# Windowed attention and a two-layer feed-forward: one more chunk's up product from seven quarter products, in a new order

## The chip, the core and the metric

The kernel runs on one core of a Trainium2 chip. The metric is the device time of one execution in microseconds (us); three runs of the kernel before took 290.29, 290.93 and 291.28, median 290.93. Engines: PE (TensorE, matrix products; its weight loads are listed as PEld), DVE (VectorE), ACT (ScalarE), POOL (GpSimd) and SP (SyncE, which here only issues DMAs). Each engine runs its own instructions in the order in which they were recorded, and waits on semaphores for the others.

## The reference

Attention over 8 batches, 8 heads, 576 positions and head size 64, where each position sees itself and the 63 before it; its output, as 4608 tokens of 512, goes through a feed-forward layer with a quick Gelu.

```python
scores = scale * np.matmul(q, k.transpose(0, 1, 3, 2))
rel = pos[:, None] - pos[None, :]
mask = (rel >= 0) & (rel < 64)
scores = np.where(mask, scores, -1e9)
attn = softmax(scores)                      # over the last axis
x = np.matmul(attn, v)                      # to [4608 tokens, 512]
h = x @ w_in                                # 512 -> 2048
g = h * (1.0 / (1.0 + np.exp(-1.702 * h)))
return (g @ w_out).astype(np.float32)       # 2048 -> 512
```

## The kernel before

**Tiling.** The 4608 tokens are 9 chunks (0 to 8) of 512, each of four blocks of 128 tokens (m = 0 to 35). A block m holds two query blocks of 64; batch b has nine of these.

**Order.** There is no loop. One long text, `plan`, lists every step by a short name, and a loop at its end calls one small function a step (table `steps`, L728). The list's order is the order of each engine's queue. A step's place among another engine's steps says nothing about its time: only the order on its own engine and the waits do.

**Attention steps.** `lb.b.i.q` (or k, v): POOL issues the load of 128 rows of q, k or v as bf16 (L227). `y.b.i.w`: SP issues a DMA transpose of such rows into `qt` or `kt` (L241; w = 0 is q, 1 is k). `h.b.i.p`: POOL shifts v by half a block into `v_off` (L234). `c.m`: scores of block m on PE (L301, matmuls L318), into the PSUM pool S or two of the pools a to d. `x.m`: exp on ACT (L326), preceded by a load of the activation table where the last function was Gelu. `m.m`: mask on DVE. `v.m.2.tag`: the products with v for blocks m and m+1 on PE (L372, L346). `n.m.2`: normalization on DVE (L383). `xd.m`: SP issues the DMA transpose of the result into `xT` (L433), the input of the feed-forward part.

**Up product, plain.** `u.ch.f.2.t0.256.tag` computes two of the sixteen 128-wide parts of h for 256 tokens: 8 matmuls of 256 columns into one PSUM bank (L441, L447). `e...` empties the bank by a Gelu on ACT (L477); a few units use `t` (tanh on ACT) and `g` (DVE) instead. In chunks 1 and 2 a unit holds four parts for 128 tokens: 16 matmuls of 128 columns.

**Up product, from seven quarter products.** Chunk 8 is computed by Strassen's scheme (with Winograd's sums). Group g = 4 ch + 2 h + k (chunk 8: 32 to 35) holds four 128x512 results: two halves of the outputs by two halves of the tokens. `F.g.n` (L645, matmuls L658) is product n, 4 matmuls of 256 columns. Products 1, 6, 7, 4 add up in one PSUM bank (`UA`), 2, 5 and 3 use another (`UB`): 5 overwrites 2, and 3 is added to 5. `K.g.n` (L670) copies `UA` after products 1, 6 and 7 to SBUF in f32, on ACT or DVE; PE's next product into that bank waits for the copy. `O.g.n` (L673) on DVE adds such a copy to `UB` after 2, 5 and 3, into one of two slots (`s_homes`, table `slots`, L638), and `G.g.n` (L680, L684) on ACT makes the Gelu of the slot, or for n = 4 of the bank itself. The sums of weights are made by `aw` (DVE, 8 of them), the sums of x by `ax.ch.n` (DVE, 4 a chunk; their places for chunks 7 and 8 are in `x_sums`, L599).

**Down product.** Chunks 1 to 8 use the same scheme for the second layer: `a` (DVE, sums of g, L529), `p.q.n` (PE, 8 matmuls of 256 columns, L543, L559; q = 2 ch + half), `k` (copy of a chain, L578), `o` (DVE, sum to the output tile, L581), `z` (last copy, L587), `s` (store, by SP or ACT, L572).

**PSUM.** Pools S and T have two banks, a to d one each. A step that names a pool waits until the last tile in it has been read.

The table of slots and the two places of the plan that matter most (L638, and from L833 on):

```python
slots = {(g, n): i % 2 for i, (g, n) in enumerate(
    ((32, 2), (33, 2), (33, 5), (32, 5), (32, 3), (33, 3))
    + ((34, 2), (35, 2), (35, 5), (34, 5), (35, 3), (34, 3)))}
```

Of the kernel before, what the change touches and what calls it, by code (L numbers as in the profile page):

```python
# [28 lines left out]
def kernel(  # L29
# [597 lines left out]
    def add_x(ch, n):  # L627
# [12 lines left out]
        for i, (g, n) in enumerate(  # L640
            ((32, 2), (33, 2), (33, 5), (32, 5), (32, 3), (33, 3))
            + ((34, 2), (35, 2), (35, 5), (34, 5), (35, 3), (34, 3))
# [81 lines left out]
    def hold(n):  # L724
# [108 lines left out]
        YY.10.0.A u.2.12.4.128.128.b w.1.0 YY.10.1.A lb.3.4.k h.2.4.0 lb.4.4.v y.2.3.1 c.12 h.3.0.0  # L833
        u.2.0.4.256.128.c u.2.8.4.256.128.b y.3.0.1 e.2.12.128 u.2.8.4.384.128.c w.3.1 e.2.0.256
        cv.2.2.2.P e.2.8.256 w.2.0 lb.3.3.q u.2.0.4.384.128.b u.2.12.4.256.128.c lb.3.4.q a.2.3
        e.2.8.384 w.4.0 e.2.0.384 e.2.12.256 w.3.0 lb.4.1.q a.2.1 u.2.12.4.384.128.b y.3.0.0 h.2.3.0
        e.2.12.384 w.1.1 a.3.3 a.3.1 lb.4.0.v a.2.2 w.2.1 a.3.2 k.2.1.A h.2.3.1 lb.3.2.v ds.0.2.S
        u.2.4.4.256.128.c u.2.4.4.384.128.b p.2.6 y.2.4.1 lb.4.0.k e.2.4.256 lb.3.3.v y.2.4.0
        p.3.1.c o.2.2.i a.2.4 y.3.1.0 k.3.1.V y.3.2.1 p.3.2.b a.3.4 lb.4.1.k e.2.4.384 p.3.6 y.3.2.0
        k.2.6.A p.2.7 c.13 x.12 o.3.2.f k.2.7.A k.3.6.V p.3.7 x.13 k.3.7.A w.4.1 p.2.4 p.3.5 m.12  # L840
        m.13 v.12.2.a z.2.A.g n.12.2 p.3.4 p.2.5 XX.12.T y.3.4.1 y.3.4.0 o.3.5.h y.3.3.1 z.3.V
# [17 lines left out]
        e.4.6.0 e.4.4.0 y.5.0.0 u.4.14.2.0.256.a e.4.12.0 u.4.0.2.0.256.d x.21 k.6.1.V x.20 p.6.6  # L859
        m.20 u.4.2.2.256.256.c k.6.6.V s.4.0.N.S h.4.1.1 y.5.0.1 s.5.0.N.S h.5.1.1 lb.5.1.q y.5.1.0  # L860
        m.21 lb.5.1.k u.4.10.2.256.256.d y.5.1.1 e.4.0.0 u.4.4.2.256.256.a y.5.2.0 e.4.14.0
        e.4.10.256 h.4.3.0 lb.5.4.k p.6.7 k.6.7.V lb.6.0.v e.4.4.256 h.4.2.0 v.20.2.d n.20.2
        e.4.2.256 c.22 x.22 m.22 p.6.4 u.4.8.2.256.256.a p.6.2.c z.6.A.g t.4.8.256 u.4.0.2.256.256.d
        o.6.2.e xd.20 p.6.5 lb.5.3.q y.5.3.0 lb.5.0.v p.7.1.b xd.21 e.4.0.256 u.4.14.2.256.256.d
        a.7.2 a.7.4 u.4.12.2.256.256.a g.4.8.256 k.7.1.A e.4.14.256 p.7.6 lb.6.1.q h.5.0.0 o.6.5
        p.6.3 k.7.6.V c.23.da s.6.1.N.S c.24 p.7.7 y.6.1.0 o.6.3 e.4.12.256 lb.6.0.q x.23 m.23
        y.6.0.0 a.8.3 lb.5.3.v h.5.0.1 y.5.4.1 k.7.7.A p.7.2.c u.5.14.2.0.256.d o.7.2.i x.24 c.25
        x.25 h.5.1.0 v.22.2.a lb.6.1.v p.7.5 lb.6.3.k n.22.2 xd.23 lb.6.1.k u.5.4.2.0.256.a e.5.14.0
        o.7.5.g xd.22 p.7.4 e.5.4.0 h.5.3.0 m.24 u.5.12.2.0.256.d e.5.12.0 u.5.10.2.0.256.a lb.6.0.k
        p.7.3 o.7.3 y.6.0.1 e.5.10.0 lb.5.2.v u.5.8.2.0.256.d e.5.8.0 y.6.1.1 u.5.6.2.0.256.a z.7.A  # L870
        s.7.1.N.S u.5.0.2.0.256.c e.5.0.0 a.8.1 p.8.1.d h.5.3.1 k.8.1.V a.8.2 m.25 u.5.2.2.0.256.b
        e.5.2.0 u.4.6.2.256.256.c h.6.1.0 s.5.1.N.S lb.6.2.k lb.6.4.k e.4.6.256 lb.6.2.v p.8.6
        k.8.6.A lb.5.4.q u.5.8.2.256.256.b a.9.3 a.9.1 u.5.12.2.256.256.c h.5.2.1 y.5.4.0 e.5.6.0
        e.5.12.256 h.5.2.0 v.24.2.a lb.7.2.k lb.6.2.q c.27 p.8.7 k.8.7.A n.24.2 lb.7.0.v xd.25 a.8.4
        e.5.8.256 a.10.3 p.9.1.c a.10.1 u.5.2.2.256.256.a k.9.1.V e.5.2.256 a.9.2 lb.7.0.q
        u.5.6.2.256.256.b x.27 t.5.6.256 lb.6.4.q p.8.4 z.8.V.g s.3.1.N.S lb.7.0.k p.8.2.a o.8.2.f
        u.5.4.2.256.256.d p.9.6 xd.24 h.6.2.1 a.9.4 p.8.5 h.6.0.0 g.5.6.256 y.6.4.1 y.7.0.0
        u.5.0.2.256.256.b o.8.5 h.6.2.0 y.6.2.1 k.9.6.V e.5.4.256 e.5.0.256 p.8.3 o.8.3 p.9.7
        k.9.7.V m.27 c.26 x.26 lb.7.1.q c.28.db m.26 s.8.1.N.S u.5.14.2.256.256.a lb.5.4.v x.28
        p.9.4 z.9.V.h a.10.2 a.10.4 e.5.14.256 u.6.6.2.0.256.d lb.7.1.k u.5.10.2.256.256.b e.6.6.0  # L880
        p.10.1.c k.10.1.V e.5.10.256 a.11.3 a.11.1 lb.6.3.q u.6.2.2.0.256.a p.9.2.d o.9.2.g h.5.4.0
        e.6.2.0 u.6.4.2.0.256.b e.6.4.0 y.7.0.1 u.6.12.2.0.256.a e.6.12.0 m.28 lb.7.2.q lb.6.3.v
        p.10.6 k.10.6.A u.6.10.2.0.256.b y.6.4.0 a.11.2 p.9.5 h.7.0.1 y.6.3.1 o.9.5 e.6.10.0 p.10.7
        k.10.7.A p.9.3 y.6.2.0 v.26.2.a c.29 x.29 c.31.bd x.31 s.6.0.N.S o.9.3 n.26.2
        u.6.8.2.0.256.a p.10.4 p.10.2.b m.29 h.6.3.0 u.6.0.2.0.256.d o.10.2.e p.10.5 z.10.V.f
        e.6.8.0 lb.6.4.v o.10.5 y.7.1.0 e.6.0.0 h.6.1.1 s.8.0.N.S h.6.0.1 v.28.2.a h.7.0.0 y.6.3.0
        c.30 y.7.1.1 c.32.cd x.32 x.30 p.10.3 lb.7.3.v n.28.2 o.10.3 m.32 xd.27 p.11.1.a aw.1.0
        lb.7.4.q u.6.14.2.0.256.c k.11.1.A aw.1.1 xd.26 m.30 e.6.14.0 a.12.3 u.6.12.2.256.256.d
        u.6.4.2.256.256.b e.6.4.256 e.6.12.256 lb.7.4.k p.11.6 k.11.6.V u.6.10.2.256.256.c
        t.6.10.256 u.6.2.2.256.256.b t.6.2.256 p.11.7 g.6.10.256 u.6.14.2.256.256.d m.31  # L890
        u.6.6.2.256.256.c s.9.0.N.S e.6.14.256 g.6.2.256 xd.29 h.6.4.0 y.7.2.1 y.7.2.0 k.11.7.V
        h.6.3.1 v.30.2.b n.30.2 s.10.0.N.S lb.7.1.v c.33 x.33 u.6.0.2.256.256.d t.6.0.256 p.11.4
        z.11.A.g p.11.2.b aw.2.0 g.6.0.256 xd.28 u.7.2.2.0.256.a u.6.8.2.256.256.d o.11.2.e h.7.3.1
        e.6.6.256 lb.7.3.k y.7.3.1 u.7.10.2.0.256.c h.7.1.1 a.11.4 p.11.5 e.7.2.0 lb.7.3.q lb.7.2.v
        lb.7.4.v h.7.2.0 m.33 y.7.4.1 h.7.1.0 v.32.2.a e.6.8.256 a.13.3 o.11.5 y.7.3.0 c.34 y.7.4.0
        c.35.dc e.7.10.0 x.34 h.7.4.0 x.35 n.32.2 p.11.3 o.11.3 u.7.0.2.0.256.a u.7.12.2.0.256.b
        e.7.12.0 u.7.4.2.0.256.d h.7.3.0 m.35 xd.31 h.7.2.1 u.7.6.2.0.256.c m.34 v.34.2.b e.7.0.0
        e.7.6.0 a.12.1 e.7.4.0 xd.30 p.12.1.a u.7.8.2.0.256.c u.7.2.2.256.256.d k.12.1.A s.11.0.N.S
        a.12.2 s.7.0.N.S xd.33 p.12.6 aw.4.0 n.34.2 u.7.6.2.256.256.b k.12.6.V p.12.7 xd.32 F.32.1.S
        F.32.2.T t.7.2.256 g.7.2.256 e.7.8.0 e.7.6.256 u.7.14.2.0.256.c aw.2.1 a.13.1 e.7.14.0  # L900
        aw.4.1 p.13.1.d k.13.1.V u.7.14.2.256.256.b u.7.12.2.256.256.c k.12.7.A p.12.4 a.12.4 a.13.2
        a.13.4 p.13.6 e.7.12.256 u.7.4.2.256.256.c e.7.14.256 aw.3.0 k.13.6.A z.12.A.e xd.35
        K.32.1.A F.33.1.b p.12.2.a xd.34 ax.8.3 ax.8.1 ax.8.2 F.32.6 O.32.2 s.10.1.N.S a.14.3 a.14.1
        K.33.1.A F.33.6 e.7.4.256 ax.8.4 o.12.2.i F.32.5 K.32.6.A p.13.7 F.32.7 p.12.5 k.13.7.V
        p.13.4 K.33.6.V F.33.7 u.7.8.2.256.256.c K.33.7.A F.33.2.d o.12.5 p.12.3 G.32.2 z.13.V.f
        s.9.1.N.S O.33.2 F.33.4 K.32.7.A o.12.3 s.12.1.N.A F.32.4 G.33.2 e.7.8.256 p.13.2.a o.13.2.h
        F.33.5 O.33.5 G.33.4 u.7.10.2.256.256.c O.32.5 e.7.10.256 p.13.5 aw.3.1 o.13.5 F.35.1.b
        K.35.1.V F.32.3 F.35.2.c G.33.5 O.32.3 G.32.4 F.33.3 G.32.5 O.33.3 p.13.3 o.13.3 s.13.1.N.A
        a.14.2 F.35.6 a.14.4 F.34.2.T G.33.3 O.35.2 F.34.1.S K.34.1.A p.14.1.d k.14.1.A G.32.3
        O.34.2 u.7.0.2.256.256.a e.7.0.256 s.12.0.N.A F.34.6 K.34.6.A K.35.6.V p.14.6 k.14.6.V  # L910
        a.15.3 a.15.1 a.15.2 p.15.1.a s.11.1.N.S F.35.7 K.35.7.A F.34.7 k.15.1.A p.14.7 K.34.7.A
        k.14.7.V G.35.2 F.35.4 G.35.4 F.34.4 G.34.4 a.15.4 p.15.6 p.14.4 G.34.2 z.14.V.e F.35.5
        p.14.2.b O.35.5 k.15.6.A p.15.7 k.15.7.A G.35.5 o.14.2.f p.14.5 o.14.5 s.14.1.N.A F.35.3
        O.35.3 G.35.3 a.16.3.0 a.16.1.0 F.34.5 O.34.5 G.34.5 p.14.3 o.14.3 p.15.2.d o.15.2.i
        a.16.3.1 a.16.1.1 a.16.2.1 p.16.1.c k.16.1.A p.15.4 s.13.0.N.A a.16.2.0 s.14.0.N.A F.34.3
        O.34.3 z.15.V.g G.34.3 a.17.3.0 p.16.2.b a.17.1.0 p.16.6 k.16.6.V a.16.4.0 p.15.5 p.17.1.S
        p.17.2.T k.17.1.A p.16.7 o.16.2.e p.16.5 a.17.3.1 o.15.5 s.15.1.N.A a.17.1.1 a.17.2.1
        a.16.4.1 p.15.3 k.16.7.A p.16.4 o.16.5.h a.17.2.0 p.17.6 o.17.2.f s.17.0.0.A z.16.A o.15.3
        s.15.0.N.A k.17.6.V p.16.3 o.16.3 s.16.1.N.A p.17.7 k.17.7.V s.16.0.N.A a.17.4.0 p.17.5
# [34 lines left out]
```

## Time and profile before

One execution was profiled:

| | |
|---|---|
| time of the profiled execution | 291.29 us |
| its span, first to last instruction | 289.6 us |
| granted clock of PE | 1.0 throughout |
| DVE, ACT, POOL busy share of the span | 68%, 65%, 46% |
| plain up product, 256 columns (L447) | 640 matmuls, 512 of them from `xT_dma` |
| down products (L559) | 896 matmuls |
| quarter products of the up product (L658) | 112 matmuls |
| Gelu from a bank (L478) | 86, mean 0.597 us |
| activation table loads | 28, each 1.28 us |

How to read it: "busy" of PE counts from the start of a matmul to the modelled end of its results, and matmuls overlap; what counts is the distance from one start to the next. On the other engines, too, an instruction's duration can be longer than the distance to the next, as the end of one overlaps the start of the next. Idle time is put down to the semaphore that ended it. A time with no other mark is counted from the first instruction of the span.

### The profile page before, as it was taken

To read this page: it belongs to the slowest core of one execution; us is meant where nothing else is said; L and a number is where in the kernel's file an instruction comes from. 1 tells how busy PE (TensorE), PEld (TensorE's weight loads), DVE (VectorE), ACT (ScalarE), POOL (GpSimd) and SP (SyncE) were. 2 spreads that over 40 slices of the span, in tenths; PEclk is the share of its full clock that TensorE was granted. 3 is DMA by queue.
4 is the path that set the end of the run, shared out by engine and by line. 5 is a ranking of instruction groups with operands and counts; after the bars stand their busy time and mean duration, and the time that the engine had idled before them with its cause. 6 is when DMAs were issued, how large, how long until landed. Compare 5 with 4: busy or idle time off the path is not lost.

```text
span 289.6 us, 8951 instructions
## 1 busy us (share of the span) xinstructions
PE 280.6 (97%) x3776; PEld 250.2 (86%) x3783; DVE 196.6 (68%) x379; ACT 187.3 (65%) x302; POOL 132.9 (46%) x185
## 2 busy tenths in 40 slices
PE   8799999999989999999999999999999999999995
PEld 7578456799989899999999999998999999999984
DVE  4767746798994695956364548564867677585963
ACT  3676537988867389774897646868979734555310
POOL 1570452879849987668379955104622000000000
PEclk9999999999999999999999999999999999999999
DMA  7999999999999999999999999555996440010223
GB/s 232 245 206 222 241 246 230 186 199 163 128 129 164 146 188 159 134 143 178 191 155 172 133 194 154 111 150 51 149 153 63 121 135 2 36 75 0 111 83 134
DMA packets 149767, 42.78 MB, mean 148 GB/s; under 512 B 135136, under 2 KB 144864, under 8 KB 149728
## 3 DMA queue, kind: packets, MB, share of 16 engines
q0 software_dynamic: 77712, 13.64, 75.7%
q1 hardware_dynamic: 68208, 25.18, 48.0%
q10 hardware_dynamic: 3808, 3.41, 3.8%
q8 instruction: 29, 0.48, 0.7%
q14 instruction: 10, 0.08, 0.1%
HBM read 36.70 MB, written 9.44 MB: 159 GB/s over the span
## 4 chain that ended last, share of the span: by engine, by line
PE 87%; DMA 7%; ACT 1%; POOL 1%; DVE 1%; issue 0%; SPq 0%; POOLq 0%
PE hps L447 37%; PE chain L559 19%; PE part L559 14%; PE up L658 4%; PE ops L485 4%; PE Tacc L346 4%; PE S L318 3%; DMA kt<-rows_k 3%; DMA stage_v<-in_v_dram 2%; DMA stage_qk<-in_k_dram 2%; PE turn L197 1%; PE pxt L414 1%; POOL v_off L117 1%; DVE PT L338 1%; POOL v_nat L117 0%; ACT L718 0%
## 5 line engine op out<-in xcount | busy, mean ns | idle before, releaser
L447 PEld LDWEIGHTS <-w_in_sb 128*128 128x128 bf16 x1312 | 109.8, 113 | 4.0
L478 ACT ACTIVATE gT<-hps 128x512 bf16<-128x512 f32 x86 | 49.7, 597 | 30.8 <-PE hps L447 30.5
L447 PE MATMUL hps<-xT_dma,w_in_sb 128*128 128x256 bf16 x512 | 62.0, 273 | 0.0
L447 PE MATMUL hps<-xT_pe,w_in_sb 128*128 128x128 bf16 (+2 forms) x800 | 60.6, 234 | 0.0
L559 PEld LDWEIGHTS <-gT 128*128 128x128 bf16 x512 | 49.4, 98 | 5.6
L583 DVE TENSOR_TENSOR o_sb<-part,stage_v 128x256 f32<-128x256 f32 x48 | 20.1, 422 | 26.1 <-PE part L559 22.2
L473 DVE SCALAR_TENSOR_TENSOR gT<-th,hps 128x512 bf16<-128x512 bf16 x42 | 28.4, 685 | 7.5 <-ACT th L458 7.4
L458 ACT ACTIVATE th<-hps 128x512 bf16<-128x512 f32 x42 | 24.7, 597 | 10.9 <-PE hps L447 10.7
L229 POOL DMA_DIRECT2D v_nat<-in_v_dram x27 | 22.8, 848 | 17.4 <-issue 17.1
L237 POOL COPY v_off<-v_nat 64x528 bf16<-64x528 bf16 x27 | 18.6, 697 | 24.7 <-DMA v_nat<-in_v_dram 24.2
L334 ACT ACTIVATE PT<-S 128x1024 bf16<-128x1024 f32 x24 | 24.4, 1016 | 4.3 <-PE S L318 4.1
L338 DVE TENSOR_TENSOR PT<-PT,band_all 128x1024 bf16<-128x1024 bf16 x32 | 23.2, 734 | 5.4 <-ACT PT L334 3.3
L117 DVE COPY stage_v<-chain 128x256 f32<-128x256 f32 x25 | 10.6, 423 | 19.2 <-PE chain L559 18.6
L232 POOL DMA_DIRECT2D rows_q<-in_q_dram x27 | 22.8, 848 | 0.0
L232 POOL DMA_DIRECT2D rows_k<-in_k_dram x27 | 22.8, 846 | 0.0
L239 POOL COPY v_off<-v_nat 64x528 bf16<-64x528 bf16 x21 | 16.3, 791 | 10.0 <-DMA v_nat<-in_v_dram 9.6
L559 PEld LDWEIGHTS <-stage_v 128*128 128x128 bf16 x192 | 18.5, 98 | 2.2
L559 PEld LDWEIGHTS <-sums 128*128 128x128 bf16 x192 | 18.5, 98 | 2.1
L391 DVE TENSOR_TENSOR xs<-Tacc,rc 128x128 bf16<-128x128 f32 (+1 forms) x26 | 18.0, 692 | 0.9
L478 ACT ACT_TABLE_LOAD x14 | 18.0, 1283 | 0.2
L117 ACT COPY stage_v<-chain 128x256 f32<-128x256 f32 x23 | 8.6, 375 | 13.0 <-PE chain L559 12.2
L718 ACT ACT_TABLE_LOAD x13 | 16.7, 1283 | 0.2
(121 smaller groups left out, 460.4 us busy)
## 6 DMA issues: line engine op xcount, KB each, us to landing
out_dram<-o_sb SPq DMA_DIRECT2D x24, 256.0 KB, 4.5
rows_k<-in_k_dram POOLq DMA_DIRECT2D x21, 128.0 KB, 5.7
rows_q<-in_q_dram POOLq DMA_DIRECT2D x21, 128.0 KB, 6.0
v_nat<-in_v_dram POOLq DMA_DIRECT2D x21, 128.0 KB, 6.0
out_dram<-o_sb ACTq DMA_DIRECT2D x10, 256.0 KB, 2.0
stage_v<-in_v_dram SPq DMA_DIRECT2D x9, 256.0 KB, 6.8
stage_qk<-in_q_dram SPq DMA_DIRECT2D x4, 512.0 KB, 6.5
stage_qk<-in_k_dram SPq DMA_DIRECT2D x4, 512.0 KB, 7.4
```

The source lines that it names most:

```text
L117: (nc.scalar.copy if engine is nc.scalar else engine.tensor_copy)(**kw)
L229: nc.gpsimd.dma_start(out=v_nat[b % 2][0 : size(i), i, :, 0:D], in_=rows_of(v, b, i))
L232: nc.gpsimd.dma_start(out=heads(row_block(b, i, w)), in_=rows_of((q, k)[w], b, i))
L237: nc.gpsimd.tensor_copy(out=vo[64:128, i, :, :], in_=vn[0:64, i, :, :])
L334: nc.scalar.activation(out=e[:], in_=st[:], func=AF.Exp, scale=scale)
L338: nc.vector.tensor_tensor(out=pt, in0=pt, in1=band_all[:], op=ALU.mult)
L447: nc.tensor.matmul(ps[:, g, :], lhsT=w_in[:, c, (f + g) % 4 : 512 : 4], rhs=xT[ch][:, m0 : m0 + nt // P, c, :], start=(c == 0), stop=(c == 3),
L458: nc.scalar.activation(out=th[:], in_=ps[:], func=AF.Tanh, scale=1.702)
L473: nc.vector.scalar_tensor_tensor(out=g_of(*unit), in0=th[:], scalar=1.0, in1=ps[:], op0=ALU.add, op1=ALU.mult,)
L478: nc.scalar.activation(out=g_of(*unit), in_=ps[:], func=AF.Gelu_apprx_sigmoid, scale=2.0)
L559: nc.tensor.matmul(out[:, :], lhsT=left[:, j], rhs=right[:, j], start=new and j == 0, stop=j == 7, skip_group_check=True,)
L583: nc.vector.tensor_tensor(out=out_half(c, pr, t, half, buf), in0=C_of[c, pr][:], in1=kept(c, pr, at), op=ALU.add)
```

## The change

1. Chunk 7's plain up product (16 units `u`, 15 of them emptied by `e` and one by `t` and `g`) is replaced by four groups (28 to 31) of seven quarter products `F`, with their 12 `K`, 12 `O`, 16 `G` and four `ax.7`. The table of slots gets the eight groups by one rule. The functions are the ones that chunk 8 uses.
2. `c.12` stands three units `u` later.
3. From chunk 4's second half on, the order of the rest of the plan is new: loads, transposes, units, products, stores, and which engine makes a copy. Two more of the early units than before go through `e` instead of `t` and `g`, chunk 7 apart; `z` stands on ACT 11 times and on DVE 5 (8 and 8 before).

The built programs differ on PE by 32 instructions: 16 matmuls and 16 weight loads fewer. ACT loads its table 24 times (28 before).

The diff, cut to its core; the first lines of the plan show `c.12`, the next the stretch around batch 7's last loads, the last the quarter products of chunk 7 and of chunk 8's first groups:

```diff
     slots = {
         (g, n): i % 2
         for i, (g, n) in enumerate(
-            ((32, 2), (33, 2), (33, 5), (32, 5), (32, 3), (33, 3))
-            + ((34, 2), (35, 2), (35, 5), (34, 5), (35, 3), (34, 3))
+            (g0 + g, n)
+            for g0 in (28, 30, 32, 34)
+            for g, n in ((0, 2), (1, 2), (1, 5), (0, 5), (0, 3), (1, 3))
         )
     }
...
-        YY.10.0.A u.2.12.4.128.128.b w.1.0 YY.10.1.A lb.3.4.k h.2.4.0 lb.4.4.v y.2.3.1 c.12 h.3.0.0
-        u.2.0.4.256.128.c u.2.8.4.256.128.b y.3.0.1 e.2.12.128 u.2.8.4.384.128.c w.3.1 e.2.0.256
+        YY.10.0.A u.2.12.4.128.128.b w.1.0 YY.10.1.A lb.3.4.k h.2.4.0 lb.4.4.v y.2.3.1 h.3.0.0
+        u.2.0.4.256.128.c u.2.8.4.256.128.b y.3.0.1 e.2.12.128 u.2.8.4.384.128.c c.12 w.3.1
...
+        y.7.2.0 c.33.da n.30.2 y.7.3.1 c.34 p.11.5 e.6.6.256 xd.29 x.33 m.33 x.34 m.34 p.12.1.c
...
+        F.29.1.b K.29.1.A F.28.2.T n.34.2 K.28.6.A o.13.2.g aw.2.1 aw.4.1 p.13.5 s.9.1.N.S k.13.7.A
+        o.13.5.e F.29.6 p.12.3 O.28.2 G.28.2 o.12.3 K.29.6.A aw.4.0 p.13.3 o.13.3 F.29.2.a O.29.2
+        F.28.7 K.28.7.A F.29.7 K.29.7.V G.29.2 F.28.5 O.28.5 F.28.4 G.28.4 F.29.5 O.29.5 G.28.5
+        G.29.5 F.31.1.c K.31.1.V F.29.4 G.29.4 F.28.3 F.29.3 xd.34 xd.35 ax.8.3 F.30.1.S K.30.1.A
+        O.29.3 G.29.3 F.31.6 F.31.2.b p.13.4 F.30.2.T F.30.6 K.31.6.A F.31.7 O.28.3 G.28.3 z.13.A
+        xd.33 xd.32 ax.8.1 K.30.6.A O.31.2 F.31.5 O.30.2 G.30.2 F.30.7 K.31.7.V O.31.5 F.33.1.a
+        F.30.5 K.30.7.A F.31.3 K.33.1.V G.31.2 O.31.3 G.31.5 F.30.4 F.31.4 G.30.4 G.31.3 G.31.4
```

## The prediction

> **What bounds the kernel now.** First the busy times at the head of the page:
>
> ```profile
> PE 280.6 (97%) x3776; PEld 250.2 (86%) x3783; DVE 196.6 (68%) x379; ACT 187.3 (65%) x302; POOL 132.9 (46%) x185
> ```
>
> PE alone is near its whole span. A matmul's modelled end overlaps the next, so this could still hide gaps; the table of waits, PE alone, lists what it waited for:
>
> ```profile
> PE idle L692 <- POOL ident L268: 1.4, 1, 1.4
> PE S L318 <- DMA kt<-rows_k: 1.0, 1, 1.0
> PE turn L148 <- DVE rows_k L117: 0.7, 1, 0.7
> PE turn L148 <- DVE rows_q L117: 0.6, 1, 0.6
> PE Tacc L346 <- POOL v_nat L117: 0.6, 1, 0.6
> ```
>
> Columns: waiter, releaser, us in total, times, longest. Only the second line lies after the start-up. The timeline of PE puts it at step `c.12`:
>
> ```profile
> 83.02 0.41 PE L318 MATMUL S<-qt,kt 64*128 64x64 bf16 x16 [1.04 <-DMA kt<-rows_k]
> 83.36 7.34 PE L447 MATMUL hps<-xT_pe,w_in_sb 128*128 128x128 bf16 x128
> ```
>
> From 83 us on PE never waits again, until its last matmuls (286.1 us); then come 3.5 us of last add and store. Two windows over that time say how much room the others have:
>
> ```profile
> 83.00:229.00 146.00, 145.98 (x2023) 135.34 (x2024) 96.03 (x184) 107.23 (x166) 88.47 (x114) 1.00 1.66 148
> 229.00:286.00 57.00, 57.00 (x523) 53.06 (x520) 39.60 (x81) 23.69 (x48) 0.00 (x0) 1.00 0.20 70
> ```
>
> (length, then busy us and count of PE, PEld, DVE, ACT, POOL; clock; DMA.) In the last 57 us, where chunk 8's quarter products lie, DVE is busy 69%, ACT 42%, and the clock is full. So whatever shortens PE's stream shortens the kernel, as long as no result reaches PE late.
>
> **What the change takes off PE.** The chain of waits runs through the quarter products, back to back:
>
> ```profile
> 252.86 1.75 PE up L658 x16
> 254.61 0.87 PE part L559 x8
> ```
>
> 16 matmuls in 1.75 us, 8 in 0.87: 0.109 us each. Chunk 7's plain up product is 16 units of 8 = 128 matmuls; four groups of seven products of 4 are 112. The built programs differ by just 16 matmuls and 16 weight loads on PE: **-1.75 us**.
>
> **The moved scores step.** `c.12` needs the transpose `y.2.3.1`, issued at 74.5 us and landed at 83.0; it goes behind `u.2.0.4.256`, `u.2.8.4.256`, `u.2.8.4.384`, each 16 matmuls of 128 columns (128 in 7.3 us, so 0.9 each). It then comes at about 81.8 + 2.7 = 84.5 us, 1.5 us after the landing: the 1.04 us wait goes. What is late next is the second unit moved ahead: it writes the bank that ACT empties in
>
> ```profile
> 82.12 0.63 ACT L478 ACTIVATE gT<-hps 128x512 bf16<-128x512 f32 x1
> ```
>
> which ends at 82.75, while PE would come at 81.83 + 0.89 = 82.72: under 0.1 us of wait. `c.12` issues no DMA and its exp comes much later, so nothing else moves. PE comes 1 us earlier to what follows; the next DMA-fed step, `c.13`, had 4.1 us between landing and use. **-1.0 us** (0 if the landing slips, -1.1 at most).
>
> **What is added beside PE.** Chunk 7 now needs, as chunk 8 does, 4 `ax`, 12 `K` and 12 `O`, and its 16 Gelus mostly read SBUF. In the new order 4 more `K` stand on DVE, 8 on ACT. The timeline of DVE prices them:
>
> ```profile
> 253.03 0.42 DVE L583 TENSOR_TENSOR o_sb<-part,stage_v 128x256 f32<-128x256 f32 x1
> 253.36 0.68 DVE L117 COPY rows_k<-up 128x512 f32<-128x512 f32 x1
> 253.96 0.68 DVE L675 TENSOR_TENSOR rows_q<-up,rows_q 128x512 f32<-128x512 f32 x1
> ```
>
> A 128x512 f32 operation lasts 0.68 but the next starts after 0.60. `O` and DVE's `K`: 16 x 0.60 = 9.6; `ax`, whose row says 0.42, 4 x 0.38 = 1.5: DVE +11.1 us. ACT: 8 x 0.5 = 4. Put into the last stretch, DVE has 39.6 + 11.1 = 50.7 us of work in 57 - 1.75 = 55.25: **92%**, in place of 69%. ACT stays under 60%. This is the change's cost, and it is hidden only while DVE's queue runs on time.
>
> Here a rule of the Trainium skill speaks against the change: "Trainium Kernel Development and Optimization", Best Practices, says that arranging TensorE's work better speeds up the products but not the emptying of PSUM. Taken whole, the stretch is emptying-bound; "VectorE: DVE Perf Modes", in its section on the TRN2 errata, gives (N+151)/0.96 ns for an f32 tensor_tensor, 0.69 us at N = 512, so by the rule 16 x 0.69 + 4 x 0.42 = 12.7, DVE at 52.3 of 55.25, 95%: no room left for any wait. By the rows' spacing it is 92%. Both stay under PE, so I keep PE as the bound and charge some waits.
>
> How many? I walked the queues by hand through the densest part, where groups 30 to 35 follow with almost nothing between. Example: from the end of `F.29.4` to `F.30.7` PE has 9 quarter products and `p.13.4`, 9 x 0.436 + 0.87 = 4.8 us. ACT has, up to the `K.30.6` that `F.30.7` waits for, `G.29.4` to `K.30.6`: four of 0.6, two of 0.63, one of 0.37, 4.0 us, behind a backlog of about 0.7 and hand-overs of 0.2: 4.9 by durations (a wait of 0.1), 4.3 by spacing (none). There are some half a dozen such places: 0 to 0.7 us together by durations. The nearest row for waits in such a stretch is chunk 8's in this trace: none. I take **+0.4 us**, ends 0 and 3.
>
> **The new order from chunk 4 on** moves loads (POOL's queue), transposes and stores (SP's) against PE. Before, scores steps after 83 us found their transposes landed 1.7 us (`c.33`) to 19 us earlier, so no wait; each gain of PE eats from that. The longest feed I find ends in `c.34`: POOL can issue `lb.7.2.v` once `v.24` has read its buffer; up to `lb.6.3.v` stand 15 loads and 9 shifts of 0.85 and 0.7 to 0.8 us, 19.5 us; then `h.6.3.0` waits for a landing (5.7 us), two more loads, `h.7.1.0` waits for another (5.7), then `lb.7.3.k` (0.85 and 5.7) and its transpose (1.3 on SP and about 4.5): 46 us counted roughly. PE's work from `v.24` to `c.34` is 46.6 us and 1.4 of mode switches. Each landing counts from its issue, so the 46 holds some 2.5 us twice: 2 to 4 us of room, as before. I take **+0.3 us**, ends 0 and 2.
>
> **Mode switches.** Going into and out of scores or PV costs PE little pieces:
>
> ```profile
> 159.86 0.63 PE Tacc L346 x32
> 160.49 0.98 PE part L559 x8
> ```
>
> 0.98 in place of 0.87, and 0.1 on entry. The new order has one such block more and one direct neighbourhood of scores and PV less: **+0.1 us**. Table loads on ACT fall from 28 to 24, off the path: 0.
>
> **Sum.** -1.75 - 1.0 + 0.4 + 0.3 + 0.1 = -1.95 us. The profiled execution took 291.29 us (span 289.6 and 1.7 around it): 289.3. It stands 0.36 above the median, 290.93, so the same sum gives about **289.0 us** by the median.
>
> **Rivals.**
> 1. *Evacuation-bound, slower.* Place: `F.28` to `F.34`. DVE is at 92% only if it never idles for more than 4.5 us in that stretch; now it idles 17.4 of 57, because most of its work waits for PE, and the two slots of `US` make `O` wait for ACT's `G`. If 9 us of that idleness stay, the stretch is 50.7 + 9 = 59.7, not 55.25: +4.5, so 290.93 - 2.75 + 4.5 + 0.1 = 292.8 us. It decides from 3.5 us of added waits on. For it: DVE, ACT and banks interlock. Against: chunk 8 does the same without a wait.
> 2. *Gains given back to the feeds.* New waits of 1.8 to 3.5 us, one or two on transposes and some on `K`: about 290.4, no measurable difference. For it: slack of 1.7 to 3 us at several scores steps, and c.12 itself is such a miss. Against: only that one of 24 missed.
> 3. *The moved step does nothing* (another wait takes its place at once, or the landing comes later): 290.0. Against: POOL and SP stand as before up to there.
> 4. *No waits at all*: -1.75 - 1.1 + 0.1 gives 288.2.
>
> That the change doesn't do what it says is excluded by the 16 missing matmuls.
>
> **Numbers.** Forecast with 4 beside it (gains of 1.4 to 2.8): 0.62. Rival 3: 0.11, still faster by 0.3%. Rival 2: 0.11, rival 1: 0.16. A kernel of this kind tells 0.3%, 0.87 us, from nothing: faster 0.73, same 0.11, slower 0.16. The range begins at rival 4 less the scatter of the runs (0.3), 287.9, and reaches into rival 1, to 291.9; the upper two thirds of rival 1 stay out. The likeliest case's own range is 288.2 to 289.6.
>
> **What will show it.** Right: no PE wait at `c.12`, PE's up groups L447 fewer by 128 matmuls and the quarter products at 224, spacing 0.109; waits of PE after 80 us together under 1 us; DVE near 90% in the last 55 us. Wrong: PE waiting for `rows_k`, `rows_q` (`K`) or a freed bank between `F.28` and `F.34`, seen in waits from ACT L117 or DVE L676 to PE; or PE waits for `kt`, `qt` at `c.25` to `c.35`. The last store's 3.5 us should stay.

## The result, and the profile after

| | before | after |
|---|---|---|
| median of 20 runs | 290.97 us | 289.52 us |
| lowest, highest | 289.81, 294.11 | 288.48, 291.80 |
| ratio to before | | 0.9943 (0.9919 to 0.9966) |
| profiled execution | 291.29 us | 289.73 us |
| its span | 289.6 us | 288.0 us |

The kernel is 0.57% faster (0.3% to 0.8%): 1.45 us by the medians, 1.66 by the ratio. The forecast was 1.95 us.

The busy times at the head of the page of the kernel after:

```profile
PE 280.4 (97%) x3767; PEld 248.8 (86%) x3767; DVE 206.3 (72%) x391; ACT 187.7 (65%) x309; POOL 133.8 (46%) x185
```

PE's busy time is nearly what it was (280.6 us), although 16 matmuls went. In the trace of the kernel before 7 matmul records are missing (3776 matmuls beside 3783 weight loads), and the figure counts modelled ends that overlap, so it can't show the gain; the distances between starts can. What PE waited for:

```profile
PE turn L148 <- DVE rows_q L117: 1.6, 1, 1.6
PE idle L693 <- POOL ident L268: 1.4, 1, 1.4
PE turn L148 <- DVE rows_k L117: 0.6, 1, 0.6
PE Tacc L346 <- POOL v_nat L117: 0.3, 1, 0.3
PE hps L447 <- DMA xT_dma<-xs: 0.3, 1, 0.3
```

The wait for `kt` at `c.12` is gone. Another stands here that the first profile before didn't have, 0.3 us for the x transposes of chunk 4. In this execution the wait for the first q cast, at the start-up, was 1 us longer than in the one before (1.6 against 0.6). It is not the change's: in later profiles it was 2.0 us in the kernel before with `c.12` moved (e1) and 0.6 us in the changed kernel with `c.12` put back (e2). The chain of waits among the quarter products (start, length, matmuls):

```profile
236.91 5.68 PE up L659 x52
242.58 0.87 PE chain L559 x8
243.46 12.43 PE up L659 x112
```

112 matmuls, 28 products, stand one behind the other in 12.43 us. At 0.109 us each they need 12.22: in the densest part of the new order PE loses 0.2 us. Most of it, 0.16 us, lies at one place, where two products start 0.59 us apart in place of 0.436:

```profile
251.64 0.60 PE L659 MATMUL up<-rows_q,kt 128*128 128x256 bf16 x4
252.23 0.60 PE L659 MATMUL up<-rows_q,qt 128*128 128x256 bf16 x4
```

And the room beside PE, in the two windows of the prediction:

```profile
83.00:229.00 146.00, 145.68 (x2003) 133.95 (x2002) 100.61 (x188) 98.91 (x159) 88.34 (x114) 1.00 1.70 148
229.00:285.00 56.00, 55.72 (x528) 52.03 (x520) 45.54 (x92) 32.69 (x64) 0.00 (x0) 1.00 0.20 67
```

DVE is busy 45.5 of 56 us, 81%, where 92% was forecast.

**Where the time went.** To set the start-up aside, PE's stream is cut at the first weight load of four steps that both kernels share: A from the first unit of chunk 0 (`u.0.0`) to the last of chunk 2 (`u.2.4` at token 384), the part in which `c.12` moved; B from there to `u.4.0` of chunk 4, same order in both; C from there to the last product, `p.17.3`, the new order. The table is in us, read from the starts in each trace. Its last column has PE's waits after 20 us: time, step, and by how much a distance between two starts exceeds the usual one, where that is more than 0.1 (at scores and PV, `c` and `v`, the figure holds the 0.1 us or so of the change of step as well; the start-up's waits are left out). There `pxt` is a transpose of x on PE, `xT` the first unit of chunk 4, `up` a unit of chunk 2, `F` a quarter product:

```
kernel (profile)            c.12   A      B      C       waits: time, at, us
before                      early  71.42  51.30  144.01  55.7 v 0.45; 81.8 c.12 1.20
before, 2nd (e8)            early  70.30  51.59  144.01  58.1 pxt 0.48; 129.6 xT 0.29
before, 3rd (e9)            early  70.56  51.30  144.01  73.1 c.11 0.86
before, 4th (e11)           early  70.57  51.51  144.01  73.1 c.10 0.76; 88.8 up 0.18
changed, c.12 back (e2)     early  70.62  51.30  142.65  73.2 c.11 0.84; 251.4 F 0.16
the same, 2nd (e10)         early  70.14  51.83  142.83  58.6 pxt 0.29; 130.0 xT 0.53;
                                                         159.4 v 0.21; 252.0 F 0.16
before, c.12 later (e1)     late   70.44  51.57  144.01  74.5 c.10 0.56; 95.1 c.13 0.36
changed                     late   70.01  51.78  142.75  130.1 xT 0.48; 252.0 F 0.16
changed, x wait moved (e7)  late   71.04  51.30  142.65  73.6 c.10 0.98; 82.9 up 0.23;
                                                         251.9 F 0.16
changed, chunk 7 plain (e5) late   70.95  51.30  144.18  73.0 c.11 1.01; 74.2 c.10 0.17
```

C is the same to 0.01 us in four profiles of the kernel before, and 142.65 to 142.83 in four of the new order. Most of the gain lies there: **1.2 to 1.4 us**. Another **0.2 us** lies behind it: from the first weight load of `p.17.3` to the end of the span are 4.65 us in the five profiles of the old order and 4.44 in the eight of the new, e3 to e6 included, to 0.01 us. A moves by up to 1.1 us and B by up to 0.5 from one profile to the next of the same kernel.

### The profile page after: what moved, and what is told of

Read it like the earlier page. It is cut to its first block, busy times and chain, and to the rows that moved or that the text cites. A ratio compares the mean times of both kernels' runs of the same rounds, so it can differ in the third digit from the quotient of the medians.

```text
span 288.0 us, 8960 instructions
## 1 busy us (share of the span) xinstructions
PE 280.4 (97%) x3767; PEld 248.8 (86%) x3767; DVE 206.3 (72%) x391; ACT 187.7 (65%) x309; POOL 133.8 (46%) x185
## 4 chain that ended last, share of the span: by engine, by line
PE 87%; DMA 5%; POOL 2%; DVE 2%; ACT 1%; SPq 1%; issue 0%; DVEq 0%
PE hps L447 32%; PE chain L559 18%; PE part L559 14%; PE up L659 9%; PE ops L485 5%; PE Tacc L346 4%; PE S L318 3%; DMA stage_qk<-in_k_dram 3%; DMA xT_dma<-xs 3%; POOL w_in_sb L249 1%; PE turn L197 1%; PE pxt L414 1%; POOL v_off L117 1%; DVE sums L539 1%; POOL v_nat L117 1%; SPq L127 0%
## 5 line engine op out<-in xcount | busy, mean ns | idle before, releaser
L447 PEld LDWEIGHTS <-w_in_sb 128*128 128x128 bf16 x1184 | 95.8, 113 | 4.4 <-issue 0.6
L478 ACT ACTIVATE gT<-hps 128x512 bf16<-128x512 f32 x73 | 41.9, 597 | 27.8 <-PE hps L447 27.5
L447 PE MATMUL hps<-xT_dma,w_in_sb 128*128 128x256 bf16 x384 | 45.9, 273 | 0.3 <-DMA xT_dma<-xs 0.3
L473 DVE SCALAR_TENSOR_TENSOR gT<-th,hps 128x512 bf16<-128x512 bf16 x39 | 26.3, 685 | 7.4 <-ACT th L458 7.2
L458 ACT ACTIVATE th<-hps 128x512 bf16<-128x512 f32 x39 | 23.0, 598 | 8.5 <-PE hps L447 8.1
L117 DVE COPY stage_v<-chain 128x256 f32<-128x256 f32 x23 | 9.7, 423 | 11.1 <-PE chain L559 10.5
L117 ACT COPY stage_v<-chain 128x256 f32<-128x256 f32 x25 | 9.3, 371 | 11.4 <-PE chain L559 10.7
L559 PE MATMUL chain<-stage_qk,gT 128*128 128x256 bf16 x128 | 16.6, 273 | 0.0
L559 PE MATMUL chain<-stage_qk,sums 128*128 128x256 bf16 x128 | 16.6, 273 | 0.0
```

What stands on the lines that cost most here:

```text
L117: (nc.scalar.copy if engine is nc.scalar else engine.tensor_copy)(**kw)
L447: nc.tensor.matmul(ps[:, g, :], lhsT=w_in[:, c, (f + g) % 4 : 512 : 4], rhs=xT[ch][:, m0 : m0 + nt // P, c, :], start=(c == 0), stop=(c == 3),
L458: nc.scalar.activation(out=th[:], in_=ps[:], func=AF.Tanh, scale=1.702)
L473: nc.vector.scalar_tensor_tensor(out=g_of(*unit), in0=th[:], scalar=1.0, in1=ps[:], op0=ALU.add, op1=ALU.mult,)
L478: nc.scalar.activation(out=g_of(*unit), in_=ps[:], func=AF.Gelu_apprx_sigmoid, scale=2.0)
L559: nc.tensor.matmul(out[:, :], lhsT=left[:, j], rhs=right[:, j], start=new and j == 0, stop=j == 7, skip_group_check=True,)
```

## The experiments

**e1: only the scores step moves.** The kernel before, with

```diff
-        ... y.2.3.1 c.12 h.3.0.0 u.2.0.4.256.128.c u.2.8.4.256.128.b ... u.2.8.4.384.128.c w.3.1
+        ... y.2.3.1 h.3.0.0 u.2.0.4.256.128.c u.2.8.4.256.128.b ... u.2.8.4.384.128.c c.12 w.3.1
```

> The kernel before with c.12 three units later and nothing else. Theory (the wait at c.12 is there in every execution, and about half of it comes back at the x transposes of chunk 4, whose landing does not move): PE's wait at c.12 gone, a wait of about 0.5 us for xT at the first unit of chunk 4, ratio to before 0.998 (0.5 to 0.6 us faster). Rival (the wait of 1.04 us was an accident of the profiled execution, as the landing of its transpose varies by microseconds): ratio 1.000. Rival (all of the wait is gained): ratio 0.9965.

Measured: 0.9984 (0.9957 to 1.001). The middle is what the first theory gave, but the interval holds 1.000 and 0.9965 as well: by time alone nothing is decided. In its profile `c.12` doesn't wait; `c.10` waits 0.56 us and `c.13` 0.36. Nor does the wait at chunk 4 appear that this theory gave.

**e2: only the scores step goes back** in the changed kernel (the same two lines, the other way).

> The changed kernel with c.12 put back ahead of the three units. Theory: a wait of up to 1 us at c.12 returns, the one at chunk 4's first unit goes; ratio to before 0.996, against 0.994 with the step moved. Rival (accident): as the changed kernel, 0.994. Rival (all counts): 0.998.

Measured: 0.9952 (0.9924 to 0.998), between the forecasts and unable to separate them. Its profile does more: `c.12` stands early and does not wait at all; `c.11`, 8 us ahead of it, waits 0.84 us for `qt`.

**e8, e9, e11: the kernel before, profiled three more times; e10: e2 once more.** No edit.

> The kernel before, profiled once more, for the wait at c.12. Theory (it is there in every execution): 0.5 to 1.2 us of PE waiting for kt or qt at c.12. Rival (it depends on when the transposes happen to land, as PE waited 0.4 to 0.8 us at the two scores steps near 74 us in three of the four experiments, and not in the two kernels' first profiles): no wait there, or one near 74 us in its place.

> The kernel before, a third profile, for the length of PE's stretch from the first up product (u.0.0) to the last unit of chunk 2 (u.2.4 at 384), in which the scores step moved. Theory (waits for the transposes there come by chance of the landings, moving c.12 only moves them): 70.0 to 71.4 us as with c.12 late, with a wait at c.10, c.11 or c.12 or none. Rival (an early c.12 costs 1 us in most executions): over 71 us with a wait at c.12.

> The changed kernel with c.12 put back, a second profile, for the same stretch. Theory: 70.0 to 71.4 us. Rival: over 71 us with a wait at c.12.

> The kernel before, a fourth profile, as e9. Theory: 70.0 to 71.4 us. Rival: over 71 us with a wait at c.12.

The timelines of PE have start, length, engine, line, operation, count, idle time before it and its releaser. The kernel before, second profile, `c.12`:

```profile
82.06 0.41 PE L318 MATMUL S<-qt,kt 64*128 64x64 bf16 x16
```

The same kernel, third profile, `c.11` and `c.10`:

```profile
73.96 0.64 PE L318 MATMUL S<-qt,kt 64*128 64x64 bf16 x32 [0.67 <-DMA qt<-rows_q]
```

No wait at `c.12` in the first of these lines; in the second the wait has come two scores steps earlier, for another transpose. Over all profiles with an early `c.12`, five of six have no wait there. A has a mean of 70.60 us in those six, and 70.61 in the four listed with a late `c.12` (70.66 with the three of e3, e4 and e6 below); A and B together 122.07 and 122.10 (122.25 with the three). Single profiles scatter by 0.4 to 0.5 us around these means, so a microsecond in most executions is excluded, a few tenths are not. The wait of 1.04 us that the forecast was built on belonged to one execution.

The landings of `y.2.3.1` say how often such a wait comes. In 13 profiles of all kernels it landed after PE had reached the early place of `c.12` in two: by 1.0 us in the first profile of the kernel before, and by 1.7 us in e1, whose late `c.12` thus saved that wait. An estimate from these, if the landing doesn't depend on the move: 2.7 us in 13 executions, 0.2 us on average. In the other eleven it landed earlier, in e9 and e11 by less than 0.1 us, and there PE had lost 0.7 us at `c.11` or `c.10` 8 us ahead.

**e7: the wait for the x transposes moved.** The changed kernel, with 0.87 us of other work for PE (`p.5.2`) put ahead of chunk 4's first units; the normalization `n.18.2`, which empties the bank that `p.5.2` writes, moves ahead with it:

```diff
-        v.18.2.c p.5.4 z.5.V.f u.4.8.2.0.256.b u.4.10.2.0.256.a u.4.2.2.0.256.d lb.5.3.k n.18.2
-        p.5.2.c s.2.1.N.S ...
+        v.18.2.c n.18.2 p.5.4 p.5.2.c z.5.V.f u.4.8.2.0.256.b u.4.10.2.0.256.a u.4.2.2.0.256.d lb.5.3.k
+        s.2.1.N.S ...
```

> The changed kernel with one down product (p.5.2) and the normalization before it moved ahead of chunk 4's first plain units, 0.87 us of work for PE while the x transposes land. Theory (what the earlier scores step gains is given back at these transposes): the wait for xT_dma of 0.3 to 0.5 us goes, ratio to before 0.9925 to 0.9935, against 0.9943. Rival (DMA jitter decides and the wait comes back at another feed): 0.994 or above.

Measured: 0.9964 (0.9936 to 0.9992), so no gain over the changed kernel: the rival. The wait at chunk 4 is gone (B 51.30), and in the same profile `c.10` waits 0.98 us. The wait that this edit was to remove, in the changed kernel:

```profile
130.65 1.03 PE L447 MATMUL hps<-xT_dma,w_in_sb 128*128 128x256 bf16 x8 [0.32 <-DMA xT_dma<-xs]
```

It appears only in profiles in which A was short (70.0 to 70.3 us in the table, and 70.01 in e4), where PE arrives early and waits here, with one exception: e3, below, has it with an A of 71.06.

**e3: the new order with chunk 7 plain.** Products 2, 5, 3, 4 of groups 28 to 31 become the plain units of 8 matmuls for the same results; products 1, 6, 7 and all their `K`, `O` and `ax.7` are left out; `G` becomes `e` in its place.

```diff
-        ... F.28.7 K.28.7.A F.29.7 K.29.7.V G.29.2 F.28.5 O.28.5 F.28.4 G.28.4 ...
+        ... e.7.2.0 u.7.4.2.256.256.T u.7.4.2.0.256.S e.7.4.0 ...
```

> The changed kernel's order with chunk 7's up product plain: its four groups' products 2, 5, 3, 4 replaced in their places by the plain units of 8 matmuls, products 1, 6, 7, the K and O steps and the four sums of x left out. Theory (PE is the bound, the products cost next to no waits): 16 matmuls of 0.109 us more, so 1.75 us or 0.6% slower than the changed kernel, ratio to before 1.000. Rival (evacuation already costs PE time among the quarter products): less than 1 us slower than the changed kernel, ratio below 0.998. Rival (the new order itself loses time): ratio above 1.002.

Measured: 294.1 us, 1.0095 (1.0062 to 1.0127), far above the theory's 1.000 and in the range of the last rival, that the new order itself loses time. The table of PE's waits tells that something else does:

```profile
PE hps L447 <- ACT gT L478: 2.4, 2, 1.2
```

Two units wait for a bank that ACT should have emptied (1.34 and 1.39 us between starts): the Gelus kept the late places that they had behind `O`. 4.4 us slower than the changed kernel are 1.75 of matmuls and 2.7 of a wait that the rewriting made. The run says nothing of the order.

**e5: the same, each Gelu right behind its unit.**

> As e3, chunk 7 plain in the changed kernel's order, but each plain unit's Gelu stands right behind its unit, so that the two waits of 1.34 and 1.39 us for a bank that e3's rewriting brought in are gone. Theory (16 matmuls more and nothing else): PE's waits for ACT gone, 1.7 to 2.0 us slower than the changed kernel, ratio to before 0.999 to 1.001, so that the new order alone brings nothing. Rival (the new order alone gains or loses): below 0.997 or above 1.003.

Measured: 1.0031 (1.0005 to 1.0058). No wait of PE after 75 us, and C is 144.18 us against 144.01 before; with the 0.2 us that its end is shorter, the new order alone brings nothing. Against the changed kernel C is 1.4 to 1.5 us longer, about the 16 matmuls less the wait of 0.16; by time the distance is 0.9%, 2.6 us, with intervals of 0.25% on each side. The time is above the 0.999 to 1.001 that was expected, and its middle just in the range of the rival that the order loses time; the profile shows no reason for it.

**e4 and e6: more work on VectorE.** The changed kernel, with a product of constants into a spare tile (128x768 bf16; it lasts 0.55 us, but in e6 the next operation starts 0.47 us after its start, not 0.55 as the expectations have it), behind every second `O` step (12) or every one (24):

```diff
+        "Q": lambda: nc.vector.tensor_tensor(out=spare[:], in0=band_all[:, 0:768], in1=band_all[:, 0:768], op=ALU.mult),
...
+        ... O.28.2 G.28.2 ... O.29.2 Q F.28.7 ...
```

> The changed kernel with 12 added operations on VectorE (a product of constants, 128x768 bf16, about 0.55 us each by the spacing, result unused), one after every second O step: 6.6 us of VectorE work among the quarter products. Theory (VectorE has about 10 us idle of 56 there, measured 45.5 busy): under 1 us slower than the changed kernel, ratio below 0.998, PE waits between the products under 1 us. Rival (VectorE decides already, each added operation comes out at PE): 4 to 6.6 us slower, ratio 1.008 to 1.017.

> The changed kernel with the added VectorE operation after every O step, 24 of them, 13 us of work. Twelve cost 1.6 us of PE time, seen as five waits for rows_q between the products. Theory (VectorE's room of 10 us of 56 is used up: from there each added operation comes out at PE): 5 to 9 us slower than the changed kernel, ratio 1.012 to 1.025. Rival (there is still slack between products): under 3 us slower, ratio below 1.005.

| added | ratio to before | C | C per added operation |
|---|---|---|---|
| 0 | 0.9943 | 142.7 us | |
| 12 | 0.9976 (0.9951 to 1.0001) | 143.99 | 0.11 us |
| 24 | 1.0163 (1.012 to 1.0205) | 147.86 | 0.32 us for each of the second twelve |

For e4 the theory was the nearer one: the ratio is below 0.998 as it said, 1.0 us above the changed kernel by time, though in C the 12 operations cost 1.3 us, not under 1; the rival's 4 to 6.6 are far off. (The 1.6 us in e6's expectation are the sum of its waits; 0.16 of them the changed kernel has too.) For e6 the theory held: 1.0163 lies in its range, 6.4 us above the changed kernel. e4's table of PE's waits names the cause, which the changed kernel's own table doesn't have (L677 is the `O` step there, L117 the copy `K`):

```profile
PE up L660 <- DVE rows_q L677: 0.4, 1, 0.4
...
PE up L660 <- DVE rows_q L117: 0.2, 1, 0.2
```

With 24, the chain of waits between 245 and 256 us no longer runs on PE at all, but on DVE, whose operations stand one behind the other:

```profile
245.01 0.55 DVE L789 TENSOR_TENSOR spare<-band_all 128x768 bf16<-128x768 bf16 x1
245.47 0.68 DVE L677 TENSOR_TENSOR rows_q<-up,rows_q 128x512 f32<-128x512 f32 x1
246.07 0.55 DVE L789 TENSOR_TENSOR spare<-band_all 128x768 bf16<-128x768 bf16 x1
```

The chain's shares by line:

```profile
by line: DVE spare L789 32.0%; DVE rows_q L677 19.4%; DVE rows_k L677 17.9%; issue 15.3%; DVE rows_k L117 7.8%; DVE rows_k L636 7.0%; DVE sums L540 5.5%; DVE rows_q L117 3.7%; DVEq L677 0.5%
```

and the last window shows DVE at 52.7 of 56 us:

```profile
229.00:285.00 56.00, 52.80 (x469) 47.68 (x465) 52.67 (x109) 32.72 (x62) 0.00 (x0) 1.00 0.16 52
```

So the forecast's slower rival exists, and stands close. By the distance between starts, which is what they take of DVE's queue, 12 operations are 5.6 us and 24 are 11.2; in the changed kernel DVE was idle for 10.5 us of the window. With 5.6 us more of DVE work the changed kernel's gain in C (1.36 us) is gone, with 11.2 DVE is the bound.

## Why the prediction was right or wrong

- **PE is the bound, 16 matmuls are 1.75 us: right.** C fell by 1.36 us in the profiles without a wait for a feed (144.01 to 142.65). Of the 0.39 us that are missing from 1.75, the wait among the products is 0.16, and 0.20 is the price of the mode switches (below). The rest is 0.04 us of longer distances within the scores, less 0.02 elsewhere.
- **The scores step, -1.0 us: wrong, and the largest error.** The step failed where it took a wait of one profiled execution for a property of the kernel. The place was right for that execution, the mechanism too (a transpose that had not landed), and the wait does go when the step moves; but five of six profiles with an early `c.12` have no wait there, and in those PE loses 0.3 to 0.9 us at `c.11`, `c.10` or the x transposes of chunk 4 instead. What the move brings on average is not told from nothing (A + B 122.07 us early, 122.10 late); the estimate by the landings is 0.2 us. The forecast's third rival, in which the moved step does nothing, is nearest to it; its time, 290.0, was still too high because it kept the next two terms.
- **Waits among the quarter products, +0.4: mis-sized, 0.16.** The walk by durations gave up to 0.7 us, by spacing none at the place that it showed, and chunk 8's row before none; the last two were the nearer.
- **Waits for the feeds in the new order, +0.3: mis-sized.** In C the changed kernel's first profile has 0.1 us at PV step `v.22`, e10 has 0.21 us there, e2 and e7 have none. `c.34`, whose feed was given 2 to 4 us of room, came 0.9 us after its last landing in the first profile: it held, with less room than said.
- **Mode switches, +0.1: mis-sized, 0.2.** C has one block of scores and PV more and one place less where scores stand right before PV. By the starts of the weight loads, where an ordinary distance is 0.11 us, that is one entry of 0.31 us and one exit of 0.15 more, and one distance of 0.15 between scores and PV and one ordinary one less. The neighbourhood saved 0.04 us of the block's 0.24, not half of it.
- **DVE at 92%: too high, 81%.** The additions were sized well: in the last window `O` rose from 8.4 to 16.6 us, `K` on DVE from 2.0 to 4.8 and `ax` from 1.6 to 2.5, 11.9 us in all by durations, some 10.3 by the distance between starts (16 x 0.60 and 2 x 0.34), which the forecast's 11.1 used. What was missed is that the new order takes work out of the same window: sums of g 14.9 to 12.8 us, copies of chains 4.7 to 2.5, and weight sums and a Gelu product 3.5 to 2.1. The sentence "put into the last stretch" treated that stretch's other work as fixed.
- **The rule that speaks against the change** (emptying of PSUM isn't sped up) is, in the words of the Trainium skill ("Trainium Kernel Development and Optimization", Best Practices), "TensorE tiling speeds up compute but not PSUM evacuation". It speaks of tiling; to carry it over to fewer products was the prediction's own step. It did not decide here, with DVE busy 81%, but e4 and e6 show that the bound by DVE is near.
- **The end of the kernel: 0 in the sum, -0.2 measured.** The forecast had the last 3.5 us stay. Up to the landing of the last store they did; from there to the end are 1.3 us before and 1.1 after, and why is open.
- **The total** came out 0.3 to 0.5 us from the forecast, and that is luck: the wrong -1.0 stood beside +0.7 us of waits that mostly did not come. What the profiles show is -1.2 to -1.4 in C and -0.2 at the end, 1.4 to 1.6 us. The ACT table loads fell from 28 to 24 as said.

## What to carry to other kernels

A wait that one profile shows for a DMA may belong to that execution: profile the same kernel two or three times, and compare lengths of equal stretches of the bounding engine's stream, before a wait is entered in a sum. Removing work from the bounding engine paid 1.2 to 1.4 of 1.75 us here, because the other engines in that stretch kept their results ahead; add dummy work on the next engine to see how much room is left. When an order is replaced, count what leaves a stretch as well as what enters it.

## What was not expected of the hardware

Where no feed is late, PE's stream is repeatable to 0.01 us over 144 us (four profiles of the old order), while the landings of transposes in the first 80 us scatter by microseconds: in four profiles of the kernel before, `y.2.3.1` was issued at 72.9 to 74.5 us and landed at 80.0 to 83.0. Work added on DVE comes out at PE gradually, not at once: of twelve operations that take 0.47 us of its queue each, 0.11 us each came out, of the next twelve 0.32.
